# An attention, Fourier mixing and feed-forward kernel on one core: the list scheduler's order replaced by a written list of operations

## The chip, the cores and the metric

The kernel runs on one core of one Trainium2 chip. The metric is device time in microseconds, the time of one launch on that core. Five sequencers issue the work: TensorE (PE, with its weight loads shown as PEld), VectorE (DVE), ScalarE (ACT), GpSimd (POOL) and SyncE (SP, which here issues nearly all DMAs). Each runs its own instructions strictly in the order of the program, and waits on semaphores for the others.

## What is computed

The reference, cut to what matters (q, k, v are 8 x 8 x 576 x 64, w_ch1 is 512 x 2048, w_ch2 is 2048 x 512):

```python
scores = (1 / np.sqrt(64)) * (q @ k.transpose(0, 1, 3, 2))
rel = pos[:, None] - pos[None, :]
scores = np.where((rel >= 0) & (rel < 64), scores, -1e9)
x = heads_joined(softmax(scores) @ v)          # 8 x 576 x 512
X = np.fft.fft(np.fft.fft(x, axis=1), axis=2)
u = x + np.real(X)
un = (u - mean(u)) / np.sqrt(var(u) + 1e-6)    # over the last axis
out = u + np.maximum(un @ w_ch1, 0.0) @ w_ch2
```

## The kernel before

The 4608 tokens are 36 tiles of 128. Five kinds of work are woven into each other:

- **Attention**, `attn_tile(T, base)`, for each of the 36 tiles. Tiles 0 to 10 ("whole") transpose keys and queries on TensorE (`pk`, `pq`, L539) and take both score halves in one operation (`psc`, L668 and L673); tiles 11 to 35 ("split") hold every number as two 16-bit halves, turn them by DMA transposes, and take the two score halves `psc` as two operations of 16 matmuls (L659). Both end with the product with the values, `pa` (L775). The matmuls of `psc` and `pa` use a part of the array each, and stand beside each other in it.
- **The Fourier mixing**, `fft(b, base)`, once per sequence (`pg` L1035 and L1043, `pz` L1088 and L1095), which writes to a buffer `md` in HBM.
- **Normalising**, `norm_tile(T, base)`: an indirect DMA on GpSimd gathers the mixed rows into `mt` (one buffer), VectorE or GpSimd adds them to `xu` (L1258 to L1261), ScalarE and GpSimd make mean and variance, and the result is turned into `uhl`, the input of the feed-forward part. For tiles 0 and 1 the turn is a TensorE transpose `pu` (L1307), and ScalarE copies it into `uhl`.
- **Weights**: 32 pieces of 512 KB arrive in 64 bits (`wd`, L1385), three VectorE instructions turn each into 32 bits (L1394, L1399, L1406), and later ScalarE and VectorE split each in two halves. Until then the first token group uses the 32-bit weights.
- **Feed-forward**, in 18 groups of 256 tokens: `ffn(c)` for groups 0 to 10 (`ph` L1507, `po` L1487, with `hh` between them), `ffn7(c)` for groups 11 to 17 (`ph` L1728, `px` and `py` L1755, `q` L1863).

None of these functions issues anything itself. Each calls `op(engine, duration, priority, function, reads, writes, ...)`, which records one operation: 3568 in all, 726 of them on TensorE. An operation may name a second engine (`alt`) on which it could run as well. `Plan.order()` (L278) then goes through a modelled time: for each engine it takes, of the operations whose inputs and buffers are there, the one that can start first, ties and near ties by priority, and for those with a second engine it takes the engine that would be done sooner. Priorities are a base per tile plus offsets from three tables, `NUDGE`, `LEAD` and `BIAS`, in which a few dozen numbers move single kinds of operations. The result is one list of operations with their engines, and the main loop (L1992) runs their functions in that order.

The main loop also fills planned pauses of TensorE: while the feed-forward part has not begun, a planned gap of over 0.8 us gets dummy matmuls into a bank `warm` (L1997), one per 0.21 us of the gap less 0.4 us.

Of the kernel before, what the change touches and what calls it, by code (L numbers as in the profile page):

```python
# [67 lines left out]
NUDGE = {  # L68
    "": {0: 14.4, 1: 16.6, 2: -0.4, 3: 15.9, 4: 69.4, 5: 25.3, 6: -12, 8: 0.2, 10: 3.8, 11: -27.5},
    "even": {14: -0.3},  # L70
    "ffn7": {16: -0.6, 232: 0.3, 1276: 3.2, 2005: 0.6, 2006: 0.7, 2047: 12.4, 2100: -0.7, 2120: 1.3, 2141: -0.3, 2145: -0.1, 2146: 0.5, 2167: 0.2},
    "first": {21: 0.8, 32: -0.1, 62: 1.2},
    "odd": {34: -2.9},
    "piece": {0: 10.6},
    "split": {3: -0.1, 25: -0.2},
}
LEAD = {
    "": (
        0,
    ),  # L80
    "even": (
        0, 0, 0, 0, 0, 0, 0, 0,
    ),
    "ffn7": (
        0, 0, 0, 0, 0, 0, 0, 0, 0, 0, 0, 0, 0, 0, 0, 0,
        0, 0,
    ),
    "norm": (
        0, 0, 0, 0, 0, 0, 0, 0, 0, 0.4, 0, 0, 0, 0, 2.6, 2.6,
        3.9, 3.9, 3.9, 4, 3.9, 4.1, 3.9, 3.9, 3.9, 3.9, 3.9, 3.9, 3.9, 3.9, 3.9, 3.9,  # L90
        3.9, 3.9, 3.9, 3.9,
    ),
    "part": (
        0.3, 0.3, 0.3, 0.3, 0.3, 0.3, 0.3, 0.3, 0.3, 0.3, 0.3, 0.3, 0.3, 0.3, 0.3, 0.3,
        0.3, 0.3, 0.3, 0.3, -1.7, 0.3, 0.3, 0.3, 0.3, 0.3, 0.3, 0.3, 0.3, 0.3, 0.3, 0.3,
    ),
    "piece": (
        0, 0, 0, 0, 0, 0, 0, 0, 0, 0, 0, 0, 0, 0, 0, 0,
        0, 0, 0, 0, 0, 0, 0, 0, 0, 0.1, 0, 0.8, 0.8, 0.8, -9.9, -9.9,
    ),  # L100
    "pre1": (
        0, 0, 0, 0,
    ),
    "prep": (
        0, 0, 0, 0,
    ),
    "scale": (
        0, 0,
    ),
    "tail": (  # L110
        0, 0, 0, 0, 0, 0, 0, 0, 0, 0, 0, 0,
    ),
    "whole": (
        0, 0, 0, 0, -1.5, -1.5, -1.5, -1.5, -2.9, -2.9, -2.9, -2.9, -2.9, -2.9, -2.9, -2.9,
        -2.9, -2.9, -2.9, -2.9, -4.6, -2.9, -2.9, -2.9, -2.9, -2.9, -2.9, -2.9, -2.9, -2.9, -2.9, -2.9,
        -2.9, -2.9, -3.1, -3.1,
    ),
}
BIAS = {
    "ffn7": {21: -0.4},  # L120
    "first": {13: -0.8},
}
# [76 lines left out]
class Op:  # L199
    __slots__ = ("eng", "dur", "lat", "fn", "deps", "outs", "prio", "wait", "ready", "allocs", "bufs", "idx", "durs", "margin", "port", "slack", "wary", "group", "lock")  # L200


class Plan:
# [13 lines left out]
    def __init__(self, rings, fifo):  # L217
        self.rings, self.fifo, self.ops, self.gaps = dict(rings), fifo, [], []
        self.slack = self.wary = 0.0
        self.begin("", 0)  # L220
# [4 lines left out]
    def op(self, eng, dur, prio, fn, reads=(), writes=(), lat=0.0, alt=(), holds=(), port=True, lock=True):  # L225
# [4 lines left out]
        lead = LEAD.get({"split": "whole", "odd": "even", "first": "even"}.get(self.kind, self.kind), ())  # L230
        prio += NUDGE.get(self.kind, {}).get(self.k, 0.0) + (lead[self.at] if self.at < len(lead) else 0.0)
        o.group = (self.kind, self.at, self.k)
        bias = BIAS.get(self.kind, {}).get(self.k, 0.0)
# [3 lines left out]
        o.margin = (alt[2] if len(alt) > 2 else self.MARGIN) + bias  # L237
# [40 lines left out]
    def order(self):  # L278
        busy = {}
        engs = sorted({e for o in self.ops for e in o.durs})  # L280
        free = {e: 0.0 for e in engs}
        avail = {e: [] for e in engs}
        slots = {r: [0.0] * n for r, n in self.rings.items()}
        for o in self.ops:
            o.wait, o.ready = len(o.deps), 0.0
            for d in o.deps:
                d.outs.append(o)
        for o in self.ops:
            if not o.wait:
                for e in o.durs:  # L290
                    avail[e].append(o)
# [10 lines left out]
        while len(res) < n:  # L302
            best = None
            for e in engs:
                t0 = free[e]
                pick, ahead = None, []
                for o in avail[e]:
# [10 lines left out]
                    if not ok:  # L318
                        continue
# [1709 lines left out]
```

## Time and profile before

| | |
|---|---|
| median of 3 runs | 948.2 us (945.15 to 948.79) |
| the profiled execution's own time | 946.62 us |
| its span, first to last instruction | 944.8 us |
| TensorE busy | 928.9 us (98%) |
| VectorE, ScalarE, GpSimd busy | 800.1, 594.5 and 313.6 us |

Busy time of TensorE counts each matmul from its start to its modelled end, and a matmul of 256 columns is shown with some 0.27 us though the next can start 0.11 us after it. So 98% busy says little of small pauses: these show in the starts of the rows. A row that begins later than the row before it, by more than its matmuls take one after the other, has lost that time. The granted clock of the core was 1.000 over the span, the upper of its two levels (1.2 and 2.4 GHz).

### The profile page before, as it was taken

Reading aid. Unit: us, or ns where it says so; the run is one execution under the profiler, and the core shown is the slowest. Engines: PE = TensorE matmul, PEld = TensorE weight load, DVE = VectorE, ACT = ScalarE, POOL = GpSimd, SP = SyncE. Lnnn points to the kernel's source line nnn. Section 1 sums busy time; section 2 is a strip of 40 time slices with the busy share of each in tenths; the row PEclk is TensorE's granted clock in tenths of the full one; section 3 lists DMA queues with packets and bytes.
Section 4 is the critical chain, followed back from the end, with each engine's and each line's share of the span. In section 5 each row is a group of like instructions: output and inputs, shape, how many; then the busy total and the mean of one; then the engine's idle time right before and its main releaser. Section 6 shows DMA issues by size and latency. Waiting matters only on the chain.

```text
span 944.8 us, 25747 instructions
## 1 busy us (share of the span) xinstructions
PE 928.9 (98%) x10193; PEld 720.3 (76%) x10193; DVE 800.1 (85%) x1922; ACT 594.5 (63%) x1545; POOL 313.6 (33%) x348
## 2 busy tenths in 40 slices
PE   8999999999999999999999999999999999999997
PEld 6776767666676676677676667676788999999997
DVE  4989988888898798897788999799988788887776
ACT  6866587787686576878686675445346554655432
POOL 1111031242444453554342254313012255554120
PEclk9999999999999999999999999999999999999999
DMA  9979963279999999999999863513111343232000
GB/s 190 304 184 260 272 131 99 63 156 188 205 211 202 194 182 214 201 198 222 178 202 202 159 142 88 134 28 81 42 45 57 63 96 76 44 85 47 18 25 24
DMA packets 313257, 130.23 MB, mean 138 GB/s; under 512 B 291624, under 2 KB 292264, under 8 KB 313136
## 3 DMA queue, kind: packets, MB, share of 16 engines
q1 hardware_dynamic: 310272, 119.53, 59.1%
q0 software_dynamic: 2720, 8.92, 3.6%
q8 instruction: 80, 1.31, 0.6%
q14 instruction: 41, 0.34, 0.1%
q10 hardware_dynamic: 144, 0.13, 0.0%
HBM read 62.85 MB, written 22.04 MB: 90 GB/s over the span
## 4 chain that ended last, share of the span: by engine, by line
PE 75%; DVE 10%; DMA 6%; issue 5%; ACT 3%; POOL 1%; SPq 1%; POOLq 0%; ACTq 0%; DVEq 0%
PE ph L1507 19%; PE po L1487 19%; PE q L1863 11%; PE py L1755 5%; PE ph L1728 4%; PE px L1755 4%; PE pa L775 3%; PE pg L1043 2%; DMA pt<-flex 2%; PE psc L659 2%; PE pz L1095 2%; DMA mt<-md,gix 1%; DVE y L810 1%; PE pp L722 1%; ACT pr L705 1%
## 5 line engine op out<-in xcount | busy, mean ns | idle before, releaser
L1507 PE MATMUL ph<-uhl,w0s 128*128 128x256 f16 (+1 forms) x2040 | 262.1, 279 | 2.3 <-DVE hh L1522 1.3
L1487 PE MATMUL po<-w1s,hh 128*128 128x512 f16 (+1 forms) x1024 | 263.3, 393 | 0.6 <-DVE hh L1522 0.3
L1507 PEld LDWEIGHTS <-w0s 128*128 128x128 f16 x1920 | 185.6, 98 | 50.1 <-issue 3.0
L1487 PEld LDWEIGHTS <-hh 128*128 128x128 f16 x960 | 91.4, 98 | 82.3 <-DVE hh L1522 1.6
L1519 ACT ACTIVATE hh<-ph 128x512 f16<-128x512 f32 x80 | 47.3, 592 | 56.3 <-PE ph L1507 50.9
L705 ACT ACTIVATE pr<-pr,nm 128x128 f32<-128x128 f32 x200 | 77.5, 391 | 1.9 <-DVE nm L694 1.8
L1246 POOL DMA_INDIRECT mt<-md,gix x34 | 42.8, 1259 | 87.4 <-DVE xu L1261 39.8
L1863 PEld LDWEIGHTS <-qbd 128*128 128x128 f16 x672 | 64.9, 98 | 7.6 <-DVE qbd L1827 0.5
L1522 DVE SCALAR_TENSOR_TENSOR hh<-ph,hh 128x512 f16<-128x512 f32 x80 | 54.7, 684 | 16.3 <-ACT hh L1519 15.8
L1863 PEld LDWEIGHTS <-kst 128*128 128x128 f16 x504 | 49.3, 98 | 5.7
L478 POOL COPY yp<-y 128x1024 uint16<-128x1024 uint16 x24 | 28.7, 1195 | 73.4 <-DVE y L810 52.2
L1827 DVE TENSOR_TENSOR flex<-flex 128x256 f32<-128x256 f32 x91 | 40.2, 442 | 14.8 <-ACT flex L1822 6.0
L694 DVE CUSTOM_DVE_ANT_0 pr<-psc,mskb 128x128 f32<-128x128 f32 x200 | 45.5, 282 | 0.6 <-PE psc L659 0.5
L1755 PEld LDWEIGHTS <-wa 128*128 128x128 f16 x750 | 45.6, 98 | 0.2
L1755 PEld LDWEIGHTS <-w0s 128*128 128x128 f16 x720 | 44.9, 98 | 0.2
L1798 ACT ACTIVATE flex<-flex 128x384 f32<-128x384 f32 x40 | 20.7, 518 | 37.2 <-DVE flex L1778 37.1
L1840 ACT CAST qbd<-flex 128x1024 f16<-128x1024 f32 x28 | 29.2, 1042 | 23.7 <-DVE flex L1827 12.9
L1728 PE MATMUL ph<-uhl,w0s 128*128 128x256 f16 x384 | 43.5, 273 | 0.0
L474 ACT COPY qbd<-qbd 64x1024 uint16<-64x1024 uint16 x40 | 41.7, 1043 | 2.7 <-DMA qbd<-flex 1.7
L478 POOL COPY yT<-py 128x1024 uint16<-128x1024 uint16 (+2 forms) x24 | 26.5, 1107 | 47.7 <-DMA py<-yp 45.0
L1863 PE MATMUL q<-w1s,qbd 128*128 128x256 f16 x336 | 41.4, 273 | 0.2 <-DVE qbd L1827 0.2
L1728 PEld LDWEIGHTS <-w0s 128*128 128x128 f16 x384 | 37.6, 98 | 5.2
(285 smaller groups left out, 2132.9 us busy)
## 6 DMA issues: line engine op xcount, KB each, us to landing
wd<-in_moe_w_ch SPq DMA_DIRECT2D x26, 512.0 KB, 5.5
out<-xu SPq DMA_DIRECT2D x34, 256.0 KB, 2.8
kn<-in_k SPq DMA_DIRECT2D x32, 256.0 KB, 3.4
qn<-in_q SPq DMA_DIRECT2D x32, 256.0 KB, 4.5
xd<-xa SPq DMA_DIRECT2D x30, 256.0 KB, 3.1
xu<-xd SPq DMA_DIRECT2D x30, 256.0 KB, 3.5
flex<-in_v SPq DMA_DIRECT2D x22, 256.0 KB, 3.8
md<-mp SPq DMA_DIRECT2D x24, 192.0 KB, 3.5
```

The lines of the kernel that those rows point to most:

```text
L474: nc.scalar.mul(out, in_, scale) if scale is not None else nc.scalar.copy(out, in_)
L478: eng.tensor_copy(out, in_)
L694: nc.vector.tensor_tensor_reduce(out=t["pr", jj][:, hp], in0=t["ps", jj][:, hp], in1=mskb[:, m : m + P], scale=-0.125, scalar=3.0e38, op0= ...
L705: nc.scalar.activation(pr, src, AF.Exp, bias=t["nm", jj][:, hp : hp + 1], scale=-1.0, accum_out=t["rc"][:, hp, jj])
L1246: nc.gpsimd.indirect_dma_start(out=mts[T], out_offset=None, in_=mds[pb][0 : HR if n < 4 else 2 * HR], in_offset=bass.IndirectOffsetOnAxis( ...
L1487: nc.tensor.matmul(t["po"][i], l_, r_, start=(f == 0 and x == 0), stop=(f == NKF - 1 and x == len(mm) - 1))
L1507: nc.tensor.matmul(ph, l_, r_, start=(x == 0), stop=(x == len(mm) - 1))
L1519: nc.scalar.activation(t["hh", pr][:, 0], ph, AF.Relu)
L1522: nc.vector.scalar_tensor_tensor(out=hh[:, 1], in0=ph, scalar=0.0, in1=hh[:, 0], op0=ALU.max, op1=ALU.subtract)
L1728: nc.tensor.matmul(ph, l_, r_, start=(x == 0), stop=(x == len(mm) - 1))
L1755: nc.tensor.matmul(to[:, x], l_(a, k_), r_(b_, k_), start=(y == 0), stop=(y == 5))
L1863: nc.tensor.matmul(t["q"][q_][:, y], l_[:, a, i, m], r_(b_, m), start=(s_ + y + m + x == 0), stop=(s_ == 3 and m == 1 and x == 2 and (y == ...
```

## The change

`Plan.order()` with its choosing, and the tables `NUDGE`, `LEAD` and `BIAS`, are gone. In their place stands `ORDER`, a tuple of 3568 numbers: the place of each operation in the order in which `op` recorded it; a negative number `n` means operation `-1 - n` on its second engine. `Plan.follow(ORDER)` goes through it once; the modelled times that it still computes serve only to place the dummy matmuls. What each operation does, its tiles and its buffers are as they were. The diff, cut to its core:

```diff
-NUDGE = {
...
-LEAD = {
...
-BIAS = {
...
+ORDER = (
+    173, 304, 3, 2, 0, 174, 8, 4, 1, 176, 178, 179, -178, 181, 182, 197, 201, 202, 196, 199, 186, 175, -201, 183,
...
+)
-    def order(self):
+    def follow(self, order):
...
+        for n in order:
+            o = self.ops[max(n, -1 - n)]
+            o.eng = list(o.durs)[n < 0]
...
-        for o, gap in zip(plan.order(), plan.gaps):
+        for o, gap in plan.follow(ORDER):
```

The order is changed nearly everywhere, by small steps: of the 726 operations on TensorE no one moves by more than 17 places, and the longest part that keeps its order has 419 of them. Of the operations with two engines, 141 go from VectorE to GpSimd and 56 back, 87 from ScalarE to VectorE and 49 back, 19 from ScalarE to GpSimd and 18 back: VectorE has 47 operations fewer, ScalarE 39 fewer, GpSimd 86 more. The dummy matmuls are 49 before and 27 now: 18, 2, 2, 2, 2, 4, 5, 2, 2, 3, 3, 2 and 2 in thirteen places before, 16, 2, 2, 4 and 3 in five places now. Three places follow; line numbers of the changed kernel are 31 higher.

SyncE's queue at the start of the program; `kn`, `qn` and `v` are attention tiles, `wd0` and `wd1` weight pieces of the first and second matrix (the number behind is the piece):

```order
L448 DMA mskb_72<-in_mask 128x384
L501 DMA kn0_99<-in_k 128x8x64
L501 DMA qn0_107<-in_q 128x8x64
L501 DMA v0_81<-in_v 128x8x64
L501 DMA kn1_138<-in_k 128x8x64
L501 DMA qn1_148<-in_q 128x8x64
L501 DMA v1_82<-in_v 128x8x64
L501 DMA kn2_184<-in_k 128x8x64
L501 DMA qn2_201<-in_q 128x8x64
L501 DMA kn3_236<-in_k 128x8x64
L501 DMA qn3_241<-in_q 128x8x64
L501 DMA kn4_282<-in_k 64x8x64 x2
```

```order
L532 DMA kn0_96<-in_k 128x8x64
L532 DMA qn0_109<-in_q 128x8x64
L479 DMA mskb_72<-in_mask 128x384
L532 DMA qn1_170<-in_q 128x8x64
L532 DMA kn1_178<-in_k 128x8x64
L532 DMA v0_81<-in_v 128x8x64
L532 DMA kn2_229<-in_k 128x8x64
L532 DMA qn2_231<-in_q 128x8x64
L532 DMA kn3_241<-in_k 128x8x64
L1416 DMA wd0_4_275<-in_moe_w_ch1 128x1024
L532 DMA v1_82<-in_v 128x8x64
L532 DMA qn3_305<-in_q 128x8x64
```

The mask now follows the first keys and queries, and a weight piece stands tenth, where the first one was seventeenth.

ScalarE's queue where the first two normalised tiles are copied into `uhl0`, just ahead of the feed-forward part (`pr` and `flex` with `psc` are exponentials of a score half, `junk` squares of a weight piece):

```order
L474 COPY yT1_910<-py6_1129 128x4x128
L705 ACTIVATE flex_79,rc7_1145<-psc7_0_1089,nm7_0_1124 128x128 x4
L705 ACTIVATE flex_79,rc7_1145<-psc7_1_1091,nm7_1_1141 128x128 x4
L474 COPY uhl0_1166<-pu0_1165 128x4x128
L474 COPY flex_79<-pp7_0_1178 128x512
L474 COPY uhl0_1166<-pu1_1187 128x4x128
```

```order
L505 COPY yT1_1037<-py5_1095 128x4x128
L505 COPY kst_80<-pk9_1122 128x512
L505 COPY uhl0_1136<-pu0_1135 128x4x128
L505 ACTIVATE qbd0_77<-pq8_1142 128x512
L505 COPY kst_80<-pk8_1149 128x512
L505 COPY uhl0_1136<-pu1_1156 128x4x128
```

The eight exponentials of tile 7 stood just ahead of the first copy; now copies alone do.

TensorE's queue in token group 3, around the products `pa` of tile 16 and the score halves of tile 18 (the first matmul of each operation):

```order
L1487 MATMUL po3_1_3635<-w1s_85,hh3_3_3993 128x512
...
L775 MATMUL pa16_4095<-v0_81,pt16_0_4011 64x64
...
L659 MATMUL psc18_0_4146<-kst_80,qbd0_77 64x128
...
L659 MATMUL psc18_1_4168<-kst_80,qbd0_77 64x128
...
L1487 MATMUL po3_0_3634<-w1s_85,hh3_3_3993 128x512
```

```order
L806 MATMUL pa16_4035<-v0_81,pt16_0_3839 64x64
...
L1518 MATMUL po3_0_3648<-w1s_85,hh3_3_3867 128x512
...
L690 MATMUL psc18_0_4093<-kst_80,qbd0_77 64x128
...
L1538 MATMUL ph3_4_4123<-uhl3_2607,w0s_84 128x256
...
L1126 MATMUL pz2_0_4137<-g2_0_3972,ds__76 97x257
...
L690 MATMUL psc18_1_4153<-kst_80,qbd0_77 64x128
```

The three stood one behind the other; now other work of TensorE stands between them. Over tiles 11 to 35, a `pa` is followed directly by a `psc` 13 times before and once now, a `psc` directly by a `pa` once before and twice now, and the 50 score halves stand in 41 unbroken runs before and in 47 now.

## Rows read from the trace of the kernel before

**Rows 1.** The page's first part: busy us (share of the span) xinstructions.

```profile
PE 928.9 (98%) x10193; PEld 720.3 (76%) x10193; DVE 800.1 (85%) x1922; ACT 594.5 (63%) x1545; POOL 313.6 (33%) x348
```

**Rows 2.** Busy time by stretch: us, then engines' busy us (xinstructions), clock, DMA, GB/s.

```profile
0.00:25.00 25.00, 21.87 (x291) 16.61 (x292) 11.12 (x23) 15.97 (x61) 3.68 (x13) 1.00 0.94 195
25.00:50.00 25.00, 23.50 (x304) 20.00 (x303) 23.58 (x44) 20.86 (x77) 5.39 (x5) 1.00 0.90 300
50.00:75.00 25.00, 24.89 (x229) 17.50 (x227) 22.13 (x56) 14.72 (x49) 2.98 (x6) 1.00 0.73 182
...
800.00:850.00 50.00, 50.00 (x672) 47.32 (x670) 42.70 (x91) 27.89 (x62) 26.70 (x29) 1.00 0.33 71
```

**Rows 3.** Timeline of PE, first 83 us: start, us, what, [idle before <-releaser].

```profile
2.09 3.97 PE L1997 MATMUL warm<-ident 128*128 128x256 f16 x18 [2.09 <-POOL ident masks.py:199]
...
9.37 0.38 PE L1997 MATMUL warm<-ident 128*128 128x256 f16 x2
9.58 0.60 PE L539 MATMUL pq<-ident,qn 128*128 128x128 f32 x4
...
41.95 0.72 PE L1997 MATMUL warm<-ident 128*128 128x256 f16 x5
43.06 0.66 PE L722 MATMUL pp<-ident,pr 128*128 128x128 f32 x4 [0.39 <-ACT pr L705]
...
79.51 0.66 PE L1307 MATMUL pu<-ident,un 128*128 128x128 f32 x4 [0.75 <-ACT flex L705]
80.00 0.38 PE L1997 MATMUL warm<-ident 128*128 128x256 f16 x2
80.90 0.66 PE L722 MATMUL pp<-ident,flex 128*128 128x128 f32 x4 [0.52 <-ACT flex L705]
...
82.24 0.66 PE L722 MATMUL pp<-ident,flex 128*128 128x128 f32 x4 [0.20 <-ACT flex L474]
```

**Rows 4.** Chain of waits, 19 to 27 us: start, us, what.

```profile
19.46 6.67 DMA wd<-in_moe_w_ch
...
26.16 0.44 DVE w0s L1394
```

**Rows 5.** Timeline of PE where packed matmuls stand among others.

```profile
284.03 1.46 PE L1487 MATMUL po<-w1s,hh 128*128 128x512 f16 x6
285.42 0.95 PE L775 MATMUL pa<-v,pt 128*64 128x64 f16 x48
286.20 1.06 PE L659 MATMUL psc<-kst,qbd 128*64 128x128 f16 x32
287.20 1.47 PE L1487 MATMUL po<-w1s,hh 128*128 128x512 f16 x6
288.50 1.47 PE L1507 MATMUL ph<-uhl,w0s 128*128 128x256 f16 x12
...
352.22 0.95 PE L775 MATMUL pa<-v,pt 128*64 128x64 f16 x48
353.10 0.86 PE L1095 MATMUL pz<-g,ds__76 97*97 97x257 f16 x6
...
356.41 1.46 PE L1487 MATMUL po<-w1s,hh 128*128 128x512 f16 x6
357.80 0.64 PE L659 MATMUL psc<-kst,qbd 128*64 128x128 f16 x16
358.37 1.48 PE L1507 MATMUL ph<-uhl,w0s 128*128 128x256 f16 x12
```

**Rows 6.** Waits of PE over the span: us in total, times, longest us.

```profile
PE ph L1507 <- DVE hh L1522: 1.3, 1, 1.3
PE ph L1507 <- DMA uhl<-up: 1.1, 2, 0.7
```

**Rows 7.** One line on both engines: duration ns min/median/max, first and last start.

```profile
L565 POOL TENSOR_TENSOR flex<-qn,flex x14: 1157/1332/1677, 128.8 to 524.9; 128x512 f16<-128x512 f32 x14
...
L565 DVE TENSOR_TENSOR flex<-qn,flex x11: 682/693/1525, 221.2 to 461.4; 128x512 f16<-128x512 f32 x11
```

More of the change, by code (lines that the diff above doesn't have):

```diff
@@ L67 @@
 C_AT = ("fh", "fh", "pt", "pt")
-NUDGE = {
[L69 to L76, printed above, removed]
-LEAD = {
[L78 to L118, printed above, removed]
-BIAS = {
-    "ffn7": {21: -0.4},
-    "first": {13: -0.8},
-}
+ORDER = (
[149 rows of a table added]
+)
 VS = 64.0
@@ L199 @@
 class Op:
-    __slots__ = ("eng", "dur", "lat", "fn", "deps", "outs", "prio", "wait", "ready", "allocs", "bufs", "idx", "durs", "margin", "port", "slack", "wary", "group", "lock")
+    __slots__ = ("eng", "dur", "lat", "fn", "deps", "outs", "prio", "wait", "ready", "allocs", "bufs", "idx", "durs", "margin", "port", "slack", "wary", "group", "lock", "free")
 class Plan:
@@ new lines, in follow @@
+        for n in order:
+            o = self.ops[max(n, -1 - n)]
+            o.eng = list(o.durs)[n < 0]
+            o.dur, o.ready = o.durs[o.eng], 0.0
+            for d in o.deps:
+                late = self.LATE[d.eng] * (o.slack if "PE" in o.durs else 0.0 if d.eng in o.durs else o.wary)
+                o.ready = max(o.ready, d.free + (self.SEM if d.eng not in o.durs or d.lat else self.SELF)[d.eng] + late)
+            locks = o.lock if o.eng == "POOL" else o.eng == "DVE" and o.port
+            st = max(free[o.eng], o.ready, port if locks else 0.0)
+            for b in o.allocs:
+                slots[b.ring].sort()
+                st = max(st, slots[b.ring].pop(0))
@@ L352, in order @@
             free[o.eng] = end
-            if o.lock if o.eng == "POOL" else o.eng == "DVE" and o.port:
+            if locks:
                 port = end
-            done = end + o.lat
-            for b in o.allocs:
-                s_ = sorted(slots[b.ring])
-                slots[b.ring] = s_[1:]
-                if b.ring in line:
-                    line[b.ring].pop()
+            o.free = end + o.lat
             for b in o.bufs:
                 b.left -= 1
-                b.free_at = max(b.free_at, done + self.SEM[o.eng])
+                b.free_at = max(b.free_at, o.free + self.SEM[o.eng])
                 if b.ring and b.left == 0:
                     slots[b.ring].append(b.free_at)
-            for x in o.outs:
-                x.wait -= 1
-                late = self.LATE[o.eng] * (x.slack if "PE" in x.durs else 0.0 if o.eng in x.durs else x.wary)
-                x.ready = max(x.ready, done + (self.SEM if o.eng not in x.durs or o.lat else self.SELF)[o.eng] + late)
-                if not x.wait:
-                    for e in x.durs:
-                        avail[e].append(x)
-            res.append((st, o))
+            res.append((o, gap))
         self.span = max(free.values())
-        self.times = [st for st, _ in res]
-        return [o for _, o in res]
+        return res
 @with_exitstack
```

70 lines of the change are left out of this document (3 added, 67 removed), and 148 rows, old and new, of the table ORDER.

## Prediction

> **What bounds the kernel now.** The first view is the page's busy times [rows 1]: TensorE 98%, VectorE 85%. Taken alone it would say that TensorE is full and that an order can give nothing. So the second view is the busy time by stretch [rows 2], with the starts of TensorE's rows beside it. From 800 to 850 us TensorE is busy for all of 50.00 us, and its rows follow each other without a hole; this holds from some 600 us to the last matmul. There nothing can be won. In the first 75 us it is not so: 21.87, 23.50 and 24.89 of 25 us, and part of that is dummy work. The third view is the timeline of TensorE in that stretch [rows 3]: the reader is to see how long each run of dummy matmuls lasts until the next real one starts, and how a row names ScalarE as what ended the wait. VectorE meanwhile has 13.9 us idle in the first stretch and only 1.4 and 2.9 in the next two [rows 2]: from 25 us on, the attention tiles and the weight pieces keep it nearly full. So **the start is bound by VectorE and ScalarE through waits of TensorE, the end by TensorE alone**; between 85 and 600 us TensorE is near full with a few named waits [rows 6].
>
> The profiled execution took 946.6 us, 1.6 under the median of 948.2 and inside the range of the three runs. The sum is made against 946.6.
>
> **The change, part by part.** The operations and their tiles stay; what moves is their order, the engine of some, and 22 dummy matmuls that go. There is no scheduling on the chip in either version, so the removal of the scheduler itself costs and gives nothing.
>
> *1. Pauses at the start.* After the first three, which wait for the first loads, ten places hold dummies. Counted from the first dummy to the start of the next real matmul they take 0.21 us (the first, 9.37 to 9.58), 1.11 (41.95 to 43.06), 0.90 (the last, 80.00 to 80.90) [rows 3], and 6.9 us in all ten. Eight more waits have no dummy; they make 3.6 us, the largest, some 0.9, ending at 79.51 and the last ending at 82.24 [rows 3]. Together 10.5 us. The new program keeps two of these places, with 4 and 3 dummies; between the 0.21 and 1.11 us of the rows I take 1.0 each, so 2.0 stays, and 8.5 is the most that can go. What would make it go can be seen in the order: the exponentials of tile 7 no longer stand ahead of the copies into `uhl0` on ScalarE, and the waits that end at 79.51 and 80.90 are on these exponentials [rows 3]. A weight piece comes tenth on SyncE instead of seventeenth, so that VectorE can start its conversions in the stretch where it has 13.9 us idle. On the other side, a weight piece takes long to land, 6.67 us from issue, and the conversion on VectorE starts only then, at 26.16 [rows 4]. VectorE runs in order: with conversions placed earlier, a piece that lands late holds up the reductions of the attention scores behind it, and TensorE waits for these. One landing that falls wholly on VectorE costs 6.7 us, against the 8.5. So the bounds are **8.5 won and, if one landing shows in full and nothing is filled, some 2 lost**; I take **6 won**, nearer to the upper end, since most of the ten places lose their dummies and the unnamed waits are small ones.
>
> *2. Broken runs of packed matmuls.* This speaks against the change. Going to or from `pa` and `psc` costs TensorE time that no wait shows. A `po` of six takes 1.30 us (287.20 to 288.50), so the `po` that begins at 284.03 has given all its matmuls by 285.33; `pa`, and the two halves `psc` behind it, then hold TensorE until 287.20, **1.87 us** [rows 5]. Alone among others, one half takes from 357.71 (356.41 and 1.30) to 358.37, **0.66 us**; `pa` alone takes 0.88 us (352.22 to 353.10) and the 0.09 us ahead of it that 285.33 to 285.42 shows, **0.97 us** [rows 5]. Separate, the three take 0.97 + 2 x 0.66 = 2.29, and so 0.42 more for two borders: 0.21 us each. The order counts the borders: `pa` before `psc` 13 times and now once (12), runs of `psc` 41 and now 47 (6), `psc` before `pa` one more (-1). 17 x 0.21 = **3.6 us lost**. TensorE is what these stretches wait for, so nothing hides it; only where it waits anyway would a border be free, so the bounds are 2.5 and 3.6. I take 3.5.
>
> *3. Waits between 85 and 600 us.* Counted from starts, eleven waits cost 6.3 us there, from one that ends at 202.94 to one that ends at 592.53; the largest is 1.3 us of idle behind VectorE's `hh`, and two of together 1.1 us wait for `uhl` [rows 6]. VectorE gets 47 operations fewer and ScalarE 39 fewer, so that what TensorE waits for there stands behind less work. But every operation in those stretches has new neighbours, and GpSimd takes about twice as long for the same: 1332 ns against 693 [rows 7]. From all of them gone (6.3 won) to twice as many (6 lost); I take **2 won**, as only a part of them hangs on VectorE.
>
> A rule of the skill bears on the 141 operations that move from VectorE to GpSimd. The row first: on VectorE the same subtraction takes 682 ns at best, 693 at the median and 1525 at worst, on GpSimd 1157, 1332 and 1677 [rows 7]; so some are held up, and by up to 0.8 us, but the median is not. The Trainium skill ("SBUF — State Buffer", section "Who interferes with whom") says that a VectorE instruction with two SBUF inputs and a GpSimd instruction that reads SBUF shut each other out for a whole instruction. Taken as the usual case it would undo the relief of VectorE, and the sum would be that of the second rival below; the median in the trace speaks for the exception.
>
> *4. From 600 us to the end.* No hole to fill [rows 2]; GpSimd gets more of the sums of the last groups, and with 26.70 of 50 us busy it has room. 0, with up to 2 lost.
>
> Sum: -6 + 3.5 - 2 + 0 = -4.5. From 946.6 that is 942.1, and I say 942.0; the same shift from the median 948.2 would be 943.7, so the answer to what a median shows lies near the border.
>
> **The rivals.**
>
> *First, slower: the path of the tokens gets longer.* The additions of the gathered rows stand on GpSimd for 7 tiles now (5, 7, 13, 16, 18, 19 and 32) and for 3 before. By [rows 7] each takes some 0.65 us longer there; behind it stand gather, statistics and the next gather on the same queue, and the one buffer `mt` holds the next tile until the addition is done. `uhl` came too late twice already, by 1.1 us in all [rows 6]. If it comes late at each of the nine starts of groups 2 to 10, by 0.65 us and one instruction of GpSimd ahead of it (1.33), that is 9 x 2.0 = 18 us less what slack the starts have; with half of it on the path, 9 lost in place of part 3's 2 won. With the gain at the start cut to 3 (a GpSimd that is in demand early too) and the 3.5 of part 2: 946.6 - 3 + 3.5 + 9 = **956**. It decides from the point where all waits between 85 and 600 us pass some 15 us. For it: most new GpSimd work lies where tokens pass. Against: seven of the nine starts show no wait now, and GpSimd is busy for a third only [rows 1].
>
> *Second, no change: the start gives back what it gains.* VectorE is the bound from 25 us on, with 4.3 us idle in 50 [rows 2]; shut out by GpSimd, or held by a late piece [rows 4], it delivers no sooner, and TensorE waits in other places, now without dummies. Then part 1 gives 1 instead of 6, part 3 nothing: 946.6 - 1 + 3.5 = **949**. The skill's rule named in part 3 would do this. For it: the stretch is full on VectorE. Against: the operations ahead of the feed-forward part are as many as before on VectorE (106 and 104 by the order), but five of the folds of the first sequence are on GpSimd now.
>
> **How the numbers follow.** Forecast 0.60, no change 0.24, slower 0.16. About half a per cent, 4.7 us, is what a measurement of this kernel can tell from none: faster is below 943.5, slower above 952.9. The forecast's own range, from the bounds of parts 1 to 3, is 935 to 947; part 1 can win more than I took, and so can part 3, so I put 0.45 of its 0.60 below 943.5 and 0.15 within. The 0.24 of the second rival are within, the 0.16 of the first are slower. So faster 0.45, same 0.39, slower 0.16. The range of 8 in 10 takes in the second rival and stops short of the first: 935 to 952.
>
> **What would show it.** Part 1: the first `ph` of the feed-forward part, a microsecond behind the row at 82.24, comes 5 to 7 us sooner, and VectorE is busier in the first 25 us than 11.12. If it comes at 82 or later, the second rival holds. Part 2: `pa` and `psc` alone at 0.97 and 0.66 us, and the stretches from 200 to 550 us longer by some 3 us where no wait is named. Part 3: fewer waits on `hh` and `uhl`; more waits on `uhl` at the starts of groups are the first rival. The forecast is wrong above all if the late stretch, which has no hole, gets some, or if the dummies' going lets TensorE fall to its slower rate: the first 18 take 0.22 us each (3.97 in all) and later ones 0.11 (9.37 to 9.58 for two) at the same granted clock of 1.00 [rows 2, 3].

## The result, and the profile after

The changed kernel takes **955.6 us** in the median of six runs (952.5 to 962.5), the kernel before beside it 946.0 (944.4 to 948.8). The ratio is 1.0106, 95% interval 1.0068 to 1.0144: about 10 us slower, where the prediction said 942.0, with 935 to 952 as its range, and faster as the likeliest sign.

The profiled execution of the changed kernel is its fastest run, 952.5 us with a span of 950.7 and a mean granted clock of 0.998; the other five took 954.3 to 962.5 us at 0.994 to 0.998. The profiled execution of the kernel before had 1.000; its other runs, as far as their clock is on record beside the experiments, had 0.994 to 1.000. Lines of the changed kernel are 31 higher than those of before. First the busy times of its page, in the columns of [rows 1]:

```profile
PE 929.3 (98%) x10171; PEld 719.3 (76%) x10171; DVE 808.1 (85%) x1851; ACT 574.6 (60%) x1541; POOL 412.7 (43%) x458
```

GpSimd got 110 instructions and 99 us more. VectorE lost 71 instructions and is busy for 8 us *more* (800.1 before). That is the first sign: work left VectorE, and its time did not go with it.

The busy time by stretch, the stretches of [rows 2]:

```profile
0.00:25.00 25.00, 20.14 (x279) 15.01 (x280) 13.41 (x22) 13.42 (x58) 9.18 (x20) 1.00 0.96 209
25.00:50.00 25.00, 21.22 (x287) 18.35 (x285) 24.45 (x40) 17.26 (x69) 8.90 (x9) 0.99 0.87 256
50.00:75.00 25.00, 25.00 (x230) 19.69 (x231) 23.54 (x48) 18.03 (x73) 9.44 (x11) 0.94 0.71 199
...
800.00:850.00 50.00, 50.00 (x699) 47.62 (x697) 39.17 (x85) 25.07 (x56) 32.07 (x34) 1.00 0.28 66
```

VectorE is fuller in all of the first 75 us, TensorE emptier in the first 50, and the granted clock, 1.00 throughout before, is 0.94 in the third stretch: for 3.4 us from 49.4 us on TensorE ran at 1.2 GHz. The late stretch is as full as it was.

The waits of TensorE over the span (engine and line, what it waited for, us in total, times, longest), to be laid beside [rows 6]:

```profile
PE po L1518 <- DVE hh L1553: 3.7, 2, 2.8
PE py L915 <- ACT flex L736: 2.8, 1, 2.8
PE warm L2028 <- POOL ident masks.py:199: 2.3, 1, 2.3
PE pq L570 <- DVE flex L509: 1.9, 1, 1.9
PE ph L1538 <- DVE hh L1553: 1.6, 3, 1.0
PE pa L806 <- DMA pt<-flex: 1.4, 1, 1.4
```

No wait for `uhl` is left. Instead there are a few long ones, two of them in the start, as its timeline shows (answering [rows 3]; the last row is the first matmul of the feed-forward part):

```profile
20.47 0.66 PE L570 MATMUL pq<-ident,qn 128*128 128x128 f32 x4 [1.87 <-DVE flex L509]
...
49.93 0.80 PE L915 MATMUL py<-ident,xu 128*128 128x128 f32 x2 [2.75 <-ACT flex L736]
...
83.89 2.43 PE L1538 MATMUL ph<-uhl,w0s 128*128 128x256 f32 x10
```

That last row began at 83.2 us before. The start, which was to give 6 us, came 0.7 us later.

**The difference as a sum.** For each matmul I take the time from its start to the next one's and subtract what is usual after a matmul of its shape (the lower quartile). What is over can be summed by size and place, of both profiled executions; the number of places stands in brackets, and a dummy counts with its usual time alone:

| us | before | after | difference |
|---|---|---|---|
| dummy matmuls | 5.3 | 2.9 | -2.4 |
| pauses of 30 to 200 ns into and out of `pa` and `psc` | 16.2 (132) | 19.6 (162) | +3.4 |
| other pauses of 30 to 200 ns | 41.0 | 42.6 | +1.6 |
| waits over 200 ns | 14.1 (28) | 18.8 (22) | +4.7 |
| of these over 1 us | 1.4 (1) | 11.8 (6) | |

The first four rows sum to +7.3; with pauses under 30 ns, -0.5, that is 6.8, against 6.3 us by which the last matmul starts later. The waits became fewer, and long. The six over 1 us end at 20.5, 49.9, 249.3, 327.9, 473.3 and 607.0 us. The table explains the 6 us between the two profiled executions; the medians lie 10 us apart, and the other runs of the changed kernel have no trace.

**What stands ahead of the long waits.** The tiles in the rows: `xe`, `yT`, `f`, `h`, and their 16-bit parts `hs` and `fs`, belong to the additions of the Fourier mixing (a fold); `v` is a 16-bit half of the values, `sw` a sum of weights for the last token groups, `hh` what the second matmul of the feed-forward part reads. A VectorE instruction is called held where it takes longer than its usual time beside GpSimd. Here is the wait of 2.8 us for `hh` that ends at 327.9 us, with VectorE first:

```profile
322.26 0.56 DVE L1007 SCALAR_TENSOR_TENSOR f<-f,xe 128x388 f32<-128x388 f32 x1
322.86 0.56 DVE L1012 TENSOR_TENSOR f<-f,xe 128x388 f32<-128x388 f32 x1
323.34 2.79 DVE L1003 TENSOR_TENSOR f<-xe 128x388 f32<-128x388 f32 x1
326.16 1.08 DVE L507 TENSOR_SCALAR fs<-f 128x388 f16<-128x388 f32 x1
327.16 0.68 DVE L1553 SCALAR_TENSOR_TENSOR hh<-ph,hh 128x512 f16<-128x512 f32 x1
```

and GpSimd in the same microseconds:

```profile
322.89 2.82 POOL L978 TENSOR_TENSOR yT<-yT 128x1156 f32<-128x1156 f32 x1
325.65 1.37 POOL L509 COPY v<-v 64x1024 uint16<-64x1024 uint16 x1
```

An addition `f` that takes 0.56 us took 2.79: it is over 0.42 us after GpSimd's addition `yT`, moved there by the change, has ended at 325.71. `hh` stands behind it, TensorE behind `hh`. Ahead of the wait for `pt` that ends at 473.3, by 20 us, a `v` of 0.69 us took 4.10:

```profile
451.78 0.69 DVE L1553 SCALAR_TENSOR_TENSOR hh<-ph,hh 128x512 f16<-128x512 f32 x1 [1.58 <-ACT hh L1550]
452.81 4.10 DVE L640 SCALAR_TENSOR_TENSOR v<-flex,v 128x512 f16<-128x512 f32 x1 [0.34 <-ACT v L638]
```

beside a chain of four GpSimd instructions, of which the change moved three there:

```profile
452.03 1.03 POOL L509 COPY v<-v 64x1024 uint16<-64x1024 uint16 x1
453.00 2.24 POOL L509 COPY yT<-py 128x1024 uint16<-128x1024 uint16 x2
455.21 1.15 POOL L767 TENSOR_TENSOR flex<-pr,flex 128x512 f16<-128x512 f32 x1
```

The chain of the trace leads from this `v` to the wait, by a DMA transpose of another tile (`uhl<-up`) and SyncE's queue (start, us, what):

```profile
456.83 0.68 DVE flex L767
...
460.01 3.61 DMA uhl<-up
...
467.83 5.41 DMA pt<-flex
```

VectorE had idle time between 464 and 468 us, so how much of the 1.4 us this one instruction costs is not shown. Held instructions stand ahead of the other four as well: a conversion of 1.63 us (0.42 free) at 17.05 us, an `f` of 2.05 at 44.7, an eviction `hs` of 1.20 (0.41 free) at 246.8, an addition `sw` of 1.64 (0.69 free) at 603.3. Summed over the trace (every VectorE instruction that is over 0.2 us longer than the lower quartile of its operation and shape), VectorE loses **46.2 us in 70 instructions before and 83.3 us in 104 after, and every one of them overlaps a GpSimd instruction**, where fewer than half of all VectorE instructions do (821 of 1922 and 885 of 1851). The other side shows in `hh`, which reads `ph` from PSUM (duration ns min/median/max):

```profile
L1553 DVE SCALAR_TENSOR_TENSOR hh<-ph,hh x80: 639/685/694, 156.3 to 677.4; 128x512 f16<-128x512 f32 x80
```

Of these 80, 41 overlap a GpSimd instruction, and none is held.

### The profile page after: what moved, and what is told of

The parts are those of the page before. It is cut to its first block, busy times and chain, and to the rows that moved or that the text cites. A ratio compares the mean times of both kernels' runs of the same rounds, so it can differ in the third digit from the quotient of the medians.

```text
span 950.7 us, 25770 instructions
## 1 busy us (share of the span) xinstructions
PE 929.3 (98%) x10171; PEld 719.3 (76%) x10171; DVE 808.1 (85%) x1851; ACT 574.6 (60%) x1541; POOL 412.7 (43%) x458
## 4 chain that ended last, share of the span: by engine, by line
PE 81%; DVE 13%; ACT 2%; issue 2%; DMA 2%; SPq 0%; POOL 0%; DVEq 0%; POOLq 0%; ACTq 0%
PE ph L1538 20%; PE po L1518 19%; PE q L1894 13%; PE py L1786 5%; PE ph L1759 4%; PE px L1786 4%; PE pa L806 3%; PE psc L690 2%; PE pz L1126 2%; PE pg L1074 2%; DVE y L841 1%; DVE hh L1553 1%; PE psc L704 1%; PE pp L753 1%; DVE flex L767 1%
## 5 line engine op out<-in xcount | busy, mean ns | idle before, releaser
L736 ACT ACTIVATE pr<-pr,nm 128x128 f32<-128x128 f32 x200 | 77.6, 392 | 11.8 <-DVE nm L725 11.7
L1277 POOL DMA_INDIRECT mt<-md,gix x34 | 39.3, 1156 | 79.9 <-DVE xu L1292 26.4
L509 POOL COPY v<-v 64x1024 uint16<-64x1024 uint16 x24 | 26.9, 1120 | 58.5 <-PE pa L806 27.0
L1858 POOL TENSOR_TENSOR flex<-flex 128x256 f32<-128x256 f32 x46 | 35.8, 779 | 33.3 <-DVE flex L1858 15.4
L1858 DVE TENSOR_TENSOR flex<-flex 128x256 f32<-128x256 f32 x66 | 31.6, 479 | 14.6 <-POOL flex L1858 7.4
L1786 PE MATMUL py<-uhl,wa 128*128 128x128 f16 x570 | 41.2, 219 | 0.0
L1894 PE MATMUL q<-wt,qbd 128*128 128x256 f16 x294 | 40.1, 273 | 0.0
```

Source lines behind the costliest of these rows:

```text
L736: nc.scalar.activation(pr, src, AF.Exp, bias=t["nm", jj][:, hp : hp + 1], scale=-1.0, accum_out=t["rc"][:, hp, jj])
L1277: nc.gpsimd.indirect_dma_start(out=mts[T], out_offset=None, in_=mds[pb][0 : HR if n < 4 else 2 * HR], in_offset=bass.IndirectOffsetOnAxis( ...
L1786: nc.tensor.matmul(to[:, x], l_(a, k_), r_(b_, k_), start=(y == 0), stop=(y == 5))
L1858: return lambda eng=nc.vector: eng.tensor_tensor(out=o, in0=a, in1=b, op=al)
L1894: nc.tensor.matmul(t["q"][q_][:, y], l_[:, a, i, m], r_(b_, m), start=(s_ + y + m + x == 0), stop=(s_ == 3 and m == 1 and x == 2 and (y == ...
```

## The experiments

Five theories. **A**: the order from 85 us on is what costs. **B**: waits no longer filled with dummies let TensorE's clock fall. **C**: VectorE instructions held by GpSimd make `hh` and its like late. **D**: the broken runs of packed matmuls cost. **E**: VectorE, lengthened as in C, sets the pace, so that a wait taken away comes back at the next place. Some texts take A or B narrower or wider, and say so. All ratios are to the kernel before, run on the same chip beside them (medians 944.6 to 946.6); after stands at 1.0106.

### Where it is lost: the two orders cut and joined

```diff
 # h_startb: the first 355 operations in the order of before, then
 # the others in the order of after; h_starta: the reverse
-ORDER = (173, 304, 3, 2, 0, ...)
+ORDER = (2, 4, 8, 173, 0, ...)
```

> The order of before for the first 355 operations (to about the start of the first FFN group, 85 us), and the order of after for the other 3213, with before's 49 dummy matmuls. Theory A (the later order is what costs: in the two traces TensorE's matmuls of the stretches 100 to 800 us start in all some 6 us later against each other, and the first FFN group starts only 0.7 us later): 951 to 953, that is 5 to 7 above the kernel before. Theory B (the start is what costs: the granted clock, which fell to 0.5 for 3.4 us at 49.4 us in the trace of after and was 1.0 throughout in before, falls more often in its other runs): 946 to 949, and a mean clock of 1.000.

> The reverse: the first 355 operations in the order of after, with its 27 dummy matmuls, the other 3213 in the order of before. Theory A: 946 to 948 (the start alone is worth +0.7), clock at or near 1.000. Theory B: 950 to 956, with a mean clock below 1.000 in most runs, as after had (0.994 to 0.998).

Measured: 965.4 us, 1.0214 (1.0185 to 1.0242), and 956.4 us, 1.0117 (1.0088 to 1.0146). The two should have shared 10 us between them and lose 31. The waits of TensorE show why; h_starta first, then h_startb:

```profile
PE po L1518 <- ACT hh L1547: 10.0, 1, 10.0
```

```profile
PE pp L753 <- ACT pr L736: 6.4, 4, 5.1
```

These fall at 104 and 98 us, at the seam. That an order cut at one place leaves the engines' queues out of step there is my reading of these two waits. So the pair fits neither theory and tells little on where the loss is; what it does tell is that neither start suits the other's rest.

### Dummies and clock

a_dum adds dummies ahead of the two long waits of the start, b_few takes them from before, each by a table of counts in the main loop:

```diff
-            if early and o.eng == "PE" and gap > WARM[0]:
-                for _ in range(int((gap - WARM[1]) / 0.21)):
+            for _ in range(WARMS.get(o.idx, 0)):
                     nc.tensor.matmul(warm, wide[:, 0:P], wide, start=True, stop=True)
+# a_dum, with the order of after
+WARMS = {176: 16, 178: 2, 181: 2, 204: 4, 475: 3, 245: 14, 282: 20}
+# b_few, with the order of before
+WARMS = {176: 18, 178: 2, 181: 2}
```

> After, with 14 dummy matmuls more ahead of the matmul that waits 1.9 us at 20.5 us and 20 more ahead of the one that waits 2.8 us at 49.9 us; nothing else is changed. Theory B (the unfilled waits let the clock fall): mean clock 1.000 in every run, median 950 to 952, spread under 2 us where after's was 10. Theory A alone (the clock is a bystander): within 1.5 us of after's median, 954 to 957.

Measured: 954.9 us, 1.0099 (1.0068 to 1.0130), 951.8 to 959.1, as forecast for a clock that is a bystander. The first `ph` began at 83.84 us, with no fall ahead of it, and at 83.89 in after, with one of 3.4 us. The clock held where the dummies are, and fell elsewhere (two stretches of a_dum, columns as above):

```profile
50.00:75.00 25.00, 23.92 (x230) 18.44 (x231) 24.24 (x50) 19.17 (x80) 10.19 (x12) 1.00 0.73 208
325.00:350.00 25.00, 22.23 (x236) 15.83 (x237) 21.86 (x54) 16.85 (x47) 9.20 (x11) 0.93 0.89 179
```

The fall comes at 328.8 us, behind the same 2.8 us wait for `hh` that left the clock alone in the profiled run of after. So falls follow long waits, though not each; the dummies take them away where they stand, and a long wait that is left brings another.

> Before, with only the first 22 of its 49 dummy matmuls (those ahead of 9 us); the other 27, at ten places from 9 to 82 us, are left out. Theory B: the clock falls below 1.000 in the mean and the time rises, 948 to 955. The step of the prediction that counted dummies as time on the path: up to 4 us faster than before, 942 to 945. If they are only filling and the clock holds without them: 946, as before.

Measured: 945.5 us, 1.0011 (0.9990 to 1.0033): no change that can be told. The clock did fall more often: five of its twelve runs had 0.997 or less and took 945.5 to 953.0 us, where the kernel before beside it had 0.997 in one run of 17 and more in all others. Where the dummies stood there is now an idle wait that ends on the same event. The row that in [rows 3] followed five dummies and 0.39 us of idle is now:

```profile
43.34 0.66 PE L754 MATMUL pp<-ident,pr 128*128 128x128 f32 x4 [1.54 <-ACT pr L737]
```

**Dummies are not time on the path; what they wait for is.** Twenty-seven of them went without gain, and without a harm to the median that can be told from its interval.

### Engines and order apart

```diff
 # a_engb: after's order, each operation on before's engine;
 # b_enga: before's order, each operation on after's engine
-    ... 831 on VectorE, 1039 on GpSimd, 1512 on GpSimd ...
+    ... 831 on ScalarE, 1039 on VectorE, 1512 on ScalarE ...
```

> The order of after and its 27 dummy matmuls, but every operation on the engine that it had in before (370 of 3568 change, 141 of them back from GpSimd to VectorE). Theory C: 944 to 951, VectorE's operations lose about as little beside GpSimd as in before (46 us in all, against 83 in after). Theory A: 953 or more.

> The reverse: the order of before with its 49 dummy matmuls, every operation on the engine that it has in after. Theory C: 950 to 957, with some 80 us lost by VectorE beside GpSimd and waits of TensorE over 1 us for VectorE. Theory A: 944 to 948, as before.

Measured: 995.8 us, 1.0526 (1.0488 to 1.0564), and 996.1 us, 1.0514 (1.0479 to 1.0549). Both theories fail alike. The losses of VectorE beside GpSimd went as C said, 56.5 us in a_engb and 87.2 in b_enga, so that they go with the engines more than with the order; and the time shows that their sum over the span foretells nothing by itself. With 370 operations on the other engine, waits over 0.2 us come to 55 and 59 us, spread over all kinds: each order seems fitted to the engines that its operations run on. The swap is too coarse; what follows changes a few operations.

### Thirteen and eight operations change their engine

In `ORDER` a number `n` below zero stands for operation `-1 - n` on its second engine. a_back makes all these changes, a_mid those below the line:

```diff
-193  203  -288 -295 -296
+-194 -204  287  294  295
 # ---- a_mid: from here on
-  -832  -1040  -1045  1512  1464  1646  -2714 -2741
+   831   1039   1044 -1513 -1465 -1647   2713  2740
```

> After, in its own order and with its 27 dummy matmuls, but thirteen operations beside its longest waits of TensorE (17, 44 to 47, 246, 323, 452 to 455 and 603 us) change their engine: eleven leave GpSimd (eight for VectorE, three for ScalarE), two evictions beside them (hs at 246.8, fs at 326.2 us) go from VectorE to ScalarE; twelve of the thirteen have by this the engine of before. Theory C (a VectorE operation that meets a running GpSimd operation is held until that is over: the f addition at 323.34 us took 2.79 us against 0.56 beside the 2.82 us yT addition on GpSimd, and its successor hh let TensorE wait 2.8 us): the waits of 2.1, 2.9, 1.1, 2.9, 1.5 and 1.2 us shrink to under 1 us each, the clock stays at 1.0, median 947 to 951. Theory A (the order is to blame whichever engine works): 953 to 957, and the waits stay or come again beside.

Measured: 954.4 us, 1.0083 (1.0055 to 1.0111). The waits that ended at 249, 473 and 607 us fell from 3.8 us to 0.9, as C said. But the start, where five operations came back to VectorE and ScalarE, was 1.4 us later (the matmul `pu` that starts at 80.7 us in after starts at 82.1), the wait at 327.9 still took 1.7 us, and a new one of 2.5 us stood at 312. So the time came out as A had it (953 to 957), while three of the waits went as C said and others came beside, as E has it. In the start GpSimd's help was worth 1.4 us in this trace: with it VectorE is held, without it VectorE has more to do.

> After, with only the eight changes of engine from 246 us on that were made in the run that changed thirteen (six operations leave GpSimd, two evictions go from VectorE to ScalarE); the start is left as in after. Theory C with the start apart (in the run with thirteen the three waits at 249, 473 and 607 us fell from 3.8 us to 0.8, and what spoilt it was that the start came 1.5 us later): 951 to 953. Theory E (a wait taken away comes back at the next place): 954 to 956.

Measured: 951.2 us, 1.0076 (1.0056 to 1.0095), as C said. VectorE ahead of the late `hh` of a_mid, where `yT` is now its own and `fs` ScalarE's:

```profile
324.73 0.56 DVE L1013 TENSOR_TENSOR f<-f,xe 128x388 f32<-128x388 f32 x1
325.21 1.39 DVE L1004 TENSOR_TENSOR f<-xe 128x388 f32<-128x388 f32 x1
326.52 1.35 DVE L979 TENSOR_TENSOR yT<-yT 128x1156 f32<-128x1156 f32 x1
327.80 0.68 DVE L1554 SCALAR_TENSOR_TENSOR hh<-ph,hh 128x512 f16<-128x512 f32 x1
```

`f` takes 1.39 us in place of 2.79 (a copy of `v` on GpSimd, 324.74 to 326.18, still holds it), `yT` adds 1.35, `fs` is gone, and TensorE's wait is 1.7 us in place of 2.9. The `v` that took 4.10 us takes its usual time:

```profile
456.42 0.69 DVE L641 SCALAR_TENSOR_TENSOR v<-flex,v 128x512 f16<-128x512 f32 x1 [2.35 <-ACT v L639]
```

The wait for `pt` at 473 us is gone. By the medians eight of 3568 operations bring back some 3 of the 10 us; the intervals overlap, so this is not shown by this run alone.

### The late pieces taken ahead

```diff
 # a_hh: places in ORDER; each operation keeps its engine
-... 1040, ... 2338, -1045, ... 2339, ...
+... 2338, 2339, 1040, ... -1045, ...
-... -832, 832, ... 2265, ...
+... 2265, -832, 832, ...
-... 2738, 2606, 2609, 2605, ...
+... 2605, 2738, 2606, 2609, ...
 # a_two: a_hh and a_mid together; a_all: and a_dum
```

> After, with three of its late FFN pieces hh taken ahead on VectorE: the one at 327.2 us ahead of the fold's additions f (with its half on ScalarE ahead of the eviction fs), the one at 248.6 us ahead of the eviction hs, the one at 606.3 us ahead of the three additions sw; every operation keeps its engine. Theory A (these pieces stand too late in the order, and no more): TensorE's waits of 2.9, 1.1 and 1.2 us go and nothing takes their place, 950 to 952. Theory E (VectorE, lengthened by what it loses beside GpSimd, sets the pace between 240 and 350 us, so that a wait taken away at one place comes back at the next): the same waits shrink, others grow behind them, 953.5 to 956.

Measured: 955.2 us, 1.0122 (1.0100 to 1.0144): nothing gained. The waits went, and came back beside:

```profile
310.17 0.60 PE L1519 MATMUL po<-w1s,hh 128*128 128x512 f16 x2 [1.89 <-DVE hh L1554]
...
330.46 0.80 PE L1539 MATMUL ph<-uhl,w0s 128*128 128x256 f16 x3 [3.25 <-DVE hh L1554]
```

This is E's forecast (953.5 to 956). VectorE is held as much as in after (81.8 us against 83.3), and the `hh` behind the first of these waits is late by two additions that take 0.75 us alone:

```profile
304.05 3.27 DVE L842 TENSOR_TENSOR y<-xa 128x256 f32<-128x256 f32 x2
```

> The eight changes of engine and the three pieces hh taken ahead, with after's own 27 dummy matmuls: the run of all three changes without its 34 further dummies. Theory B (unfilled waits of 2 us and more let the clock fall, and that costs): mean clock 0.995 to 0.998, 950.5 to 952.5. If the clock is a bystander: 948 to 950.

> The eight changes of engine, the three pieces hh taken ahead and the 34 dummy matmuls at 20.5 and 49.9 us, all in one. If the waits are separate costs, they add: 947 to 950 with the clock at 1.000. Theory E: no better than the best of its parts, 952 to 955.

Measured: a_two 949.4 us, 1.0047 (1.0028 to 1.0066), a_all 948.8 us, 1.0055 (1.0036 to 1.0075). Here E fails: once the eight engine changes are made, the three pieces taken ahead pay. The two edits together bring back **half of the loss** or a little more, and a_two's interval lies just below after's. The 34 further dummies bring the clock to 1.000 in five of six runs of a_all (0.999 in the other; 0.994 to 0.998 in a_two) and no time that can be told, though the two intervals would hide 2 us. **B falls as the main cause**: with a steady clock 4 to 5 us are still lost. It does not fall altogether. After's mean clock of 0.996 over 951 us is, as an estimate, at most 3.8 us of TensorE's work; and the kernel before has the same tie between clock and time: of its 65 runs beside the experiments the 47 at 0.999 or 1.000 have a median of 944.8 us, the 11 at 0.997 or less one of 948.2. Whether the falls cost this or go with longer waits in the same runs is not shown.

### More work on GpSimd in the kernel before

```diff
 # b_pool: before's order, the second addition (yT) of seven folds on GpSimd
-563   814   1039   1309   1534   1801   2046
+-564 -815 -1040 -1310 -1535 -1802 -2047
```

> Before, in its own order, with one change of engine seven times: the second addition of each of the seven folds from 100 us on (yT, 128 x 772 or 128 x 1156 elements, 0.95 to 1.4 us on VectorE) runs on GpSimd. Theory C: the additions f or xe behind it on VectorE are held until GpSimd is through, 1 to 2.2 us each; VectorE's loss beside GpSimd rises from 46 us by 7 to 15, TensorE's waits for VectorE grow, 947 to 952. The rival, by which the prediction counted work moved to GpSimd as relief: VectorE is 7 to 9 us less busy and the time is 944 to 946.

Measured: 947.8 us, 1.0041 (1.0025 to 1.0056), slower, and VectorE's loss beside GpSimd rose from 46.2 to 58.7 us, by 12.5. Its busy time went *up*, 805.4 us for seven instructions fewer, against 800.1. One of the seven places, GpSimd and then VectorE:

```profile
468.03 2.43 POOL L979 TENSOR_TENSOR yT<-yT 128x1156 f32<-128x1156 f32 x1
```

```profile
467.58 0.68 DVE L817 TENSOR_TENSOR xa<-pa,rc 128x512 f32<-128x512 f32 x1
468.29 2.80 DVE L842 TENSOR_TENSOR y<-xa 128x256 f32<-128x256 f32 x2
```

Two additions `y` that take 0.75 us in before took 2.80, while `xa` ahead of them had its usual 0.68. The holding is C by itself, in the other kernel: moving the addition relieved VectorE of 1.35 us and held it for 2. What C said of TensorE's waits did not come: those over 0.2 us sum to 14.5 in the profiled run, as before, and the longest is one of 2.4 us for `uhl`. So the move costs time, and by which wait it does is not shown.

### Broken runs

```diff
 # a_join: the PE order of after; the first of two neighbouring runs
 # moves back to the second, at fourteen places, as for tile 17:
-psc (17, first half)  po  pz  psc (17, second half)
+po  pz  psc (17, first half)  psc (17, second half)
 # a_best: a_all, and the second moves ahead to the first, 22 times
-psc (17, first half)  po  pz  psc (17, second half)
+psc (17, first half)  psc (17, second half)  po  pz
 # b_split: before, eighteen runs broken
-psc (13, first half)  psc (13, second half)  ph
+psc (13, first half)  ph  psc (13, second half)
```

Such a broken run in the trace of after, in the columns of [rows 5]:

```profile
276.56 0.64 PE L690 MATMUL psc<-kst,qbd 128*64 128x128 f16 x16
277.13 1.47 PE L1518 MATMUL po<-w1s,hh 128*128 128x512 f16 x6
278.44 1.48 PE L1126 MATMUL pz<-g,ds__76 97*96 97x257 f16 x12
279.85 0.64 PE L690 MATMUL psc<-kst,qbd 128*64 128x128 f16 x16
```

> After, with fourteen of its broken runs of the packed score and value matmuls joined again, as they stood in before: the first of two neighbouring runs moves 2 to 3.6 us later, to the head of the second, and what depends on it moves behind. Theory D (each broken run costs TensorE a change of its mode of work: the pauses of 30 to 200 ns sum to 62.2 us in after, 57.2 in before): these pauses fall by 2.5 to 3.5 us, and the median to 952 to 953.5. If the breaks are paid for by something else: the pauses of 30 to 200 ns stay within 1 us of after's, or the scores come later and longer waits eat the gain, 954 to 957.

Measured: 958.7 us, 1.0122 (1.0088 to 1.0155), longer than either side said. The pauses into and out of packed matmuls fell from 19.6 to 16.7 us, by the 2.9 that D said; waits over 0.2 us rose from 18.8 to 24.6, above all for `hh`, 8.9 us in place of 5.3, and `pt`.

> Before, with eighteen of its joined runs of packed score and value matmuls broken: the matmul group that follows such a run goes ahead of the run's last piece, which makes twelve runs more (69 to 81; after has 86). Nothing else moves. Theory D (each broken run costs some 0.2 us at its two borders, on the path): the pauses into and out of packed matmuls rise from 16.2 us by 2 to 3, and the time by as much, to 947 to 948.5 where before takes 945 to 946. If TensorE has slack there: the pauses rise, the time stays within 0.7 us.

Measured: 946.9 us, 1.0020 (1.0005 to 1.0035), 1.8 us slower in the median, with the pauses up by 2.65 us (16.2 to 18.85). The profiled run itself, 945.1 us, had 3.5 us less of waits over 0.2 us than the profiled run of before, so the price in time is read from the median alone, and its interval goes from 0.5 to 3.3 us: **a broken run costs some 0.2 us in pauses, and at least a part of that is on the path**.

> The run of all three changes (eight engines, three pieces hh, 34 dummies), and 22 pieces of packed matmuls taken ahead by 1.3 to 5.9 us to the run before them, only such whose inputs had been ready for at least 0.3 us by then in the trace of after: 86 runs become 65, where before has 69. Theory D: the pauses into and out of packed matmuls fall from 19.7 to 15.5 us, and the time from 948.8 to 944 to 945.5, level with before or just under it. Theory E (something else then holds TensorE at the same place): 947 to 950.

Measured: 953.8 us, 1.0098 (1.0070 to 1.0127), 4 to 5 us slower than a_all and beyond both forecasts. The pauses fell by 4.8 us, to 14.9, and the waits over 0.2 us rose from 10.2 to 18.8. What took their place, in TensorE's waits of a_best:

```profile
PE pa L807 <- DMA pt<-flex: 2.7, 2, 2.2
PE psc L691 <- DVE qbd L510: 2.5, 1, 2.5
...
PE ph L1539 <- DVE hh L1554: 1.8, 1, 1.8
```

Inputs that lay ready for 0.3 us in one trace lay ready no more in the next, 5 us earlier overall. Two of the joined kinds, `pa` and `psc`, wait for 5.2 us: at such places a break is paid for by readiness, since TensorE did something else there while the input came.

No version here beats the kernel before.

## Why the prediction was wrong, step by step

**What bounds the kernel**: held in the main. The late stretch is full in both from 800 to 850 us, the start and the middle wait for VectorE and ScalarE.

**Part 1, the start (6 won; nothing found).** This is the main step that failed: the term of 6 us for the pauses at the start. The first `ph` came at 83.9 us, 0.7 later than before, which the prediction had named as the mark of its second rival; dummies, pauses and waits of the first 100 us sum to 33.9 us in after and 34.6 before. The step counted the ten dummy places, 6.9 us, as time that mostly goes when the dummies go. b_few took 27 dummies from before, and the median stayed: a dummy fills a wait, and the wait belongs to what it waits for. The order's own gain came, but small: the waits that ended at 79.5 and 80.9 us, 0.9 and 0.7 us by the sum's measure, are one of 0.5 in after. Against it stand nine waits over 0.3 us that make 8.3 us, two of them 2.1 and 2.9. The step had seen the danger in a weight piece that lands late; no wait of VectorE in the first 100 us names a weight's DMA. What the step itself left out was GpSimd, 9.18 us busy in the first 25 us against 3.68. VectorE was busier there, 13.41 against 11.12, as forecast, but part of that is holding: the conversions at 17.05 us took 1.63 and 1.09 us beside GpSimd's `v` and `y`, and 0.42 and 0.69 in a_back, where GpSimd is idle then. The lower bound of the step, "some 2 lost", does not come out of its numbers either: 8.5 less 6.7 is some 2 won, and a landing with nothing filled would be 6.7 lost.

**Part 2, broken runs (3.5 lost; 3.4 found).** Right in the pauses, to a tenth, and at least in part on the path by b_split. That it can't be had back by joining the runs again (a_join, a_best) the step did not say.

**Part 3, waits between 85 and 600 us (2 won; 1.5 lost).** This step failed too. Eleven waits of 6.5 us by the sum's measure (the prediction counted 6.3) became eight of 8.0. Their number fell, as a shorter queue of VectorE would have it, but the queue was not shorter: 47 operations fewer there, and 37 us more of holding over the whole span. The error lies in how [rows 7] was read. The median of a VectorE subtraction, 693 ns against 682 at best, was taken to mean that holding is the exception. It is; but the exceptions make 46 us in before, and they fall where GpSimd is busy, so they grew with the work that was moved there. What they add is 37 us for the 86 operations that GpSimd has more in after, 0.4 us each, and 12.5 us for the seven additions of b_pool, 1.8 each; the price that the step took from the median was nothing. The Trainium skill ("SBUF — State Buffer", section "Who interferes with whom") had said it outright: a VectorE instruction with two SBUF inputs and a GpSimd instruction that reads SBUF exclude each other for a whole instruction. The trace agrees in both directions: 2.79 us for an `f` of two SBUF inputs, and 0.694 at most for the 80 `hh` that read PSUM, 41 of them beside running GpSimd work. The program had said it as well: the removed `Plan.order()` kept one modelled time `port` (L299, L320, L353 of the kernel before) for the VectorE operations marked `port` and the GpSimd operations marked `lock`, so that the two did not overlap in its plan when it chose order and engine. `follow` still computes that time, but chooses nothing by it. Whether this alone is why before loses less was not tried.

**Part 4, from 600 us (0, up to 2 lost; 1.7 lost).** Three waits make 2.0 us against 0.4, the largest the 1.2 behind the sums `sw` at 607 us; within the bounds, though the late stretch, which had no hole, got some.

**The range.** The bounds of parts 1 to 3 as they stand add up to 934 and 958 us (946.6 less 12.3; and 946.6 with 2, 3.6 and 6 more). The 947 at the upper end of the forecast's own range is not their sum, and the 952 was set to take in the second rival and stop short of the first; with the whole sum the median of 955.6 would have lain inside.

**The rivals.** The first, slower at 956 by late tokens, has the right time and the wrong place: no wait for `uhl` is left in after, so its time is luck. The second, no change, has the right mechanism, shut out by GpSimd, and named its page; its sum of 949 stopped at the start giving 1 in place of 6 and the middle nothing. With the measured parts in their place, 946.6 - 0.7 + 3.4 + 1.5 + 1.7 gives 952.5, the profiled run; this is bookkeeping over the same two traces, with small terms left out, and no test of the rival. The remaining 3 us to the median are runs with a mean clock of 0.994 to 0.998. The prediction's last sentence had the fall of the clock by the dummies' going as a way to be wrong: the falls did come, b_few has more of them and a_all nearly none, and what they cost is not shown. Whether those runs take longer by the clock, or have longer waits and so the clock, stays open.

**What is left.** a_two brings back some 5 us of the 10 by twelve operations, eight that change their engine beside held VectorE instructions and the three `hh` taken ahead, one with its half on ScalarE; neither edit alone is shown to do it, by the intervals of a_mid and a_hh. Some 2 to 3 us may be the broken runs, as an estimate by b_split's price. The rest, about 2 us, can't be placed by these runs; the clock is one candidate.

## What to carry to other kernels

Work moved from VectorE to GpSimd was relief here only as far as VectorE read PSUM or waited meanwhile: sum what VectorE's instructions lose beside GpSimd, which a median hides, and look first at what TensorE waits for behind a held one. Dummy matmuls were no time to be won: ask what the wait that they fill is for. Take an order and the engines of its operations as one design, since half of each was worse than either (995 us); and expect a wait taken away alone to come back at the next place while the engine behind it is held as before.

## What was not expected of the hardware

VectorE can be held through several GpSimd instructions in a row: 4.10 us for a `v` of 0.69, until a chain of four had ended (GpSimd 452.03 to 456.36, `v` 452.81 to 456.91). Behind a wait of 2.8 us the clock fell to 1.2 GHz in one run (at 328.8 us in a_dum) and stayed at 2.4 in another at the same place (327.9 us in after); the fall in after's trace, at 49.4 us, lasted 3.4 us. And a pause into or out of the packed matmuls costs 0.12 us each (19.6 us for 162, 16.2 for 132), whichever kernel it stands in.
